# The gMLP's spatial part of a gated S4 and gMLP kernel: tokens instead of features on partitions, and an order of instructions that is written out

## The chip, the core and the metric

The kernel runs on one core of one Trainium2 chip, in bfloat16 with float32 accumulation in PSUM. The metric is the device time of one execution in microseconds, as the median of three runs. The engines are named as the profile names them: PE (TensorE, with its weight loads apart as PEld), DVE (VectorE), ACT (ScalarE), POOL (GpSimd) and SP (SyncE, which here only issues transfers).

## The reference

Two mixers read the same x of 2048 tokens by 640 features, and a gate for each token mixes what they give:

```python
def _A_ref(u, ...):                       # S4: a long convolution
    P = exp(dt * A * l)                   # 640 features x 128 states x 2048 positions, complex
    K = einsum('dn,dnl,dn->dl', C, P, dt * B).real
    y = irfft(rfft(pad(u)) * rfft(pad(K)))[:2048]
    return y + u * Dskip

def _B_ref(x, w_in, w_sp, b_sp, w_out):   # gMLP
    z = gelu(x @ w_in)                    # 2048 x 1728
    z1 = z[..., :864]
    z2 = layernorm(z[..., 864:])
    g = einsum('ts,bsf->btf', w_sp, z2) + b_sp[None, :, None]
    return (z1 * g) @ w_out               # 2048 x 864 by 864 x 640

g = sigmoid((x * gate_w).sum(-1, keepdims=True))
out = g * a + (1 - g) * b
```

The change is in the last three lines of `_B_ref` and in the half of z that is z1: w_sp is 2048 by 2048, b_sp has one number for each token, and z1 and g are 2048 by 864.

## The kernel before, in words

**How the order of instructions comes about.** The kernel first describes its work as some 1,700 tasks, with `Plan.add`: a task has one or several engines that may do it, a planned cost, the data it reads and writes, and the buffers it holds. `Plan.run` then plays the tasks through by these costs: whenever an engine comes free, it takes the task of the highest priority (the longest chain of planned costs that still hangs on it, plus a bias) whose inputs are ready and whose buffers are free. A table `TUNE` adds further biases to single calls. The result is one list of tasks, each with its engine. The instructions are issued in the order of this list, so each engine's queue is in order and has this fixed sequence; semaphores between engines follow from the data. The same holds for the queues of transfers, SP's and POOL's: a transfer whose data aren't ready holds up those behind it in its queue.

**Buffers.** PSUM has three rings of two buffers: `two` for pairs of banks (products of z1 and z2, the table products ps_k, the wide products of the convolution), `x` (ps_o, ps_s1x, ps_v) and `g` (ps_g, some ps_u). The rings in SBUF that matter here are wT (2), z1t (2), vT (4), br (2), ob (2) and zt (2, the staging of z1).

**The stages, with their lines in the profile.**

- x is loaded transposed; the z2 half of `x @ w_in` comes first (`z2_tile`, L592, tokens on partitions, two products of 432 columns for each slice of 128 features of x), with gelu and the layernorm's statistics on ACT and DVE. The normalised z2n stays in SBUF: 16 tiles of 128 tokens by 864 features.
- `z1_tile` (L624) makes z1 with features on partitions: for a group of 512 tokens, pairs of feature tiles of 128 (the last is 96), so products of 512 columns with the weights w_in as the stationary operand. ACT applies the gelu, and z1 goes to DRAM (z1_d) in two pieces for each pair, one for each block of 256 tokens. Of the four groups of 512 tokens two are made early, two between the tables of the S4 kernel.
- `s1_u` (L651, L655) is the first stage of the Fourier transform of u; its output goes from PSUM by copies (L422) to SBUF and to DRAM.
- `k_exps` and `k_tables` make, for eight slices of 80 features, tables of powers of the exponentials: angles on DVE and POOL (L361, L968, L993), sines and exponentials on ACT (L415), products on DVE (L1017 to L1028). `k_sub` (L1045, L1046) contracts each slice's tables over the 128 states in 160 small products ps_k; `k_store` and `k_expand` write the kernel K to DRAM and read it back widened.
- `conv_s1` (L1134, ps_s1k) transforms K, after the sixth ps_k for the first 480 features and after the eighth for the other 160. `conv_s2` multiplies the two spectra: ps_u (L1181) and ps_s2k (L1188) on PE, their product p on DVE (L1190, 32 wide ones of 2 x 480 columns, 16 narrow ones of 2 x 320), ps_v (L1196) on PE, and a copy on ACT (L1198). `conv_vt` (L1204) turns the result in 32 by 32 blocks with 16 transposes on DVE; `conv_i2` (L1278) ends the inverse transform. There the output is put together by L1212 on DVE (`stt`: gate times PSUM plus b) or by ACT and an addition (L1229, L1231), and stored.
- `sp_block(tb)`, for eight blocks of 256 tokens, is the spatial part. Two blocks are described ahead of the tables, two after them, four before `conv_s2`; where they run is up to the planned order, which fills PE's gaps with them.

**The spatial part before.** w_sp's rows for 256 tokens are loaded transposed into wT (16 slices of 128 source tokens by 256). Features are on partitions: for each of seven feature tiles, 16 products accumulate ps_g over the source tokens, with a tile of z2n as the stationary operand and 256 columns of wT as the moving one:

```python
pe.matmul(ps()[0:fs, ft - f0, :], lhsT=z2n[:, st, 128 * ft:128 * ft + fs], rhs=wT()[:, st, :], ...)      # L812
vec.tensor_tensor(out=v_, in0=ps, in1=br()..., op=ALU.add)                                                # L816
vec.tensor_tensor(out=v_, in0=v_, in1=z1t()..., op=ALU.mult)                                              # L818
```

b_sp varies along the columns here, so it is read as a row that is repeated over the partitions (br, loaded from a small table br_d in DRAM), and VectorE needs two operations for each pair of feature tiles, an addition from PSUM (L816) and a product with z1 (L818), 32 of each. Their result vT already has features on partitions and is the stationary operand of the last product ps_o (L832, 7 feature tiles, twice 320 columns for each 128 tokens). ps_o is scaled by 1 - gate into ob on DVE or ACT (L361, L836) and stored to DRAM (ob_d), or for the last four tiles of tokens kept in SBUF (acc).

## Time and profile before

| | |
|---|---|
| runs | 357.02, 362.8 and 356.61 us, median 357.02 |
| profiled execution | span of 353.6 us from the first to the last instruction |
| PE | 309.6 us busy in 3231 instructions, 88% of the span |
| DVE | 286.4 us in 548, 81% |
| ACT | 241.8 us in 437, 68% |
| POOL | 153.6 us in 155, 43% |
| ps_g, L812 | 896 instructions of 256 columns, 106.8 us of PE busy |
| L816 | 32 additions on DVE with 18.7 us busy |
| ps_o, L832 | 224 instructions of 320 columns, 34.3 us of PE busy |
| transfers | 59.89 MB, mean 169 GB/s |
| mean granted TensorE clock | 0.972 of full speed |

The page counts an engine as busy while at least one of its instructions is under way. On PE these overlap: the mean of one product in its group is the time from its start to its end, not the time from one product to the next. The page gives the span of the profiled execution; a run's time is the device's, and the three above are of other executions.

### The profile page before, as it was taken

How to read it: one execution, taken by the hardware profiler on the slowest of the kernel's cores; microseconds unless marked ns; L12 is line 12 of the kernel's file. 1: busy time of each engine (PE TensorE's matmuls, PEld its weight loads, DVE VectorE, ACT ScalarE, POOL GpSimd, SP SyncE). 2: the span in 40 equal slices, each digit the busy share in tenths (PEclk: the TensorE clock that was granted, in tenths of full speed). 3: DMA queues.
4: the chain of work that ended last, by engine and by line, in shares of the span. 5: the costliest groups of instructions: out<-in, count | busy, mean ns of one | idle time of the engine just before them, and what ended most of it. 6: DMA issues, size and time to landing. Idle time of an engine off the chain costs nothing.

```text
span 353.6 us, 8393 instructions
## 1 busy us (share of the span) xinstructions
PE 309.6 (88%) x3231; PEld 216.9 (61%) x3237; DVE 286.4 (81%) x548; ACT 241.8 (68%) x437; POOL 153.6 (43%) x155
## 2 busy tenths in 40 slices
PE   3899899989899999999699998699999999809982
PEld 3455445857778687878577776477774444405751
DVE  4079996789897949998489758777789999996985
ACT  1658975999784676889876684564538888804842
POOL 3005544600095826773187989434459400203221
PEclk9999999999999999999899999899999999977998
DMA  7988999669981578496592249998958886273404
GB/s 200 205 141 230 199 188 213 193 154 191 249 135 49 135 173 164 114 223 104 152 250 82 61 63 174 197 264 267 230 161 250 222 238 195 61 211 138 141 28 130
DMA packets 110809, 59.89 MB, mean 169 GB/s; under 512 B 78322, under 2 KB 107354, under 8 KB 110770
## 3 DMA queue, kind: packets, MB, share of 16 engines
q1 hardware_dynamic: 108530, 55.33, 63.9%
q0 software_dynamic: 2240, 4.04, 5.4%
q8 instruction: 25, 0.41, 0.5%
q14 instruction: 14, 0.11, 0.1%
HBM read 25.25 MB, written 19.47 MB: 126 GB/s over the span
## 4 chain that ended last, share of the span: by engine, by line
PE 44%; DVE 24%; ACT 10%; issue 7%; DMA 6%; POOL 5%; SPq 2%; ACTq 0%; DVEq 0%; POOLq 0%
PE ps_g L812 13%; DVE p L1190 5%; DVE vs L1204 5%; PE ps_z L592 5%; PE ps_o L832 4%; PE ps_z L624 4%; DMA xf<-in_A_u_dram 4%; PE ps_s2k L1188 3%; POOL ci L361 3%; PE ps_k L1045 3%; PE ps_v L1196 3%; PE ps_k L1046 3%; PE ps_s1k L1134 2%; ACT z2n L596 2%; ACT ET L415 2%
## 5 line engine op out<-in xcount | busy, mean ns | idle before, releaser
L812 PE MATMUL ps_g<-wT,z2n 128*128 128x256 bf16 (+1 forms) x896 | 106.8, 276 | 5.8 <-issue 2.8
L812 PEld LDWEIGHTS <-z2n 128*128 128x128 bf16 (+1 forms) x896 | 90.2, 103 | 22.7 <-issue 8.7
L1190 DVE TENSOR_TENSOR p<-ps_s2k,us 128x960 bf16<-128x960 f32 (+1 forms) x48 | 48.4, 1040 | 1.9 <-PE ps_s2k L1188 0.6
L361 POOL TENSOR_SCALAR ci<-ai 128x640 int32<-128x640 int32 (+1 forms) x8 | 21.5, 2693 | 55.3 <-DVE ai L968 33.2
L361 POOL TENSOR_SCALAR si<-th 128x80 int32<-128x80 f32 x40 | 32.1, 802 | 12.7 <-DVE t3p L761 4.6
L832 PE MATMUL ps_o<-Wout,vT 128*128 128x320 bf16 (+1 forms) x224 | 34.3, 299 | 3.0 <-ACT ob L836 3.0
L624 PE MATMUL ps_z<-xg,Win 128*128 128x512 bf16 (+1 forms) x134 | 31.6, 380 | 0.8 <-ACT zt L415 0.5
L592 PE MATMUL ps_z<-Win,xT 128*128 128x432 bf16 (+1 forms) x160 | 30.4, 346 | 2.1 <-ACT gl L598 2.1
L415 ACT ACTIVATE ET<-ci 128x640 bf16<-128x640 int16 (+1 forms) x40 | 26.0, 677 | 6.9 <-POOL ci L361 3.5
L832 PEld LDWEIGHTS <-vT 128*128 128x128 bf16 (+1 forms) x224 | 21.8, 98 | 13.5 <-issue 4.1
L1045 PE MATMUL ps_k<-ET 128*32 128x33 bf16 x640 | 27.7, 259 | 1.6 <-DVE ET L1028 1.1
L1045 PEld LDWEIGHTS <-ET 128*32 128x32 bf16 x640 | 26.9, 193 | 3.6 <-DVE ET L1028 3.1
L1198 ACT CAST vs<-ps_v 128x480 bf16<-128x480 f32 (+1 forms) x48 | 24.3, 521 | 5.1 <-PE ps_v L1196 4.1
L1046 PE MATMUL ps_k<-ET 128*32 128x33 bf16 x640 | 27.6, 258 | 0.0
L1046 PEld LDWEIGHTS <-ET 128*32 128x32 bf16 x640 | 27.1, 195 | 0.3 <-issue 0.3
L816 DVE TENSOR_TENSOR vT<-ps_g,br 128x512 bf16<-128x512 f32 (+1 forms) x32 | 18.7, 615 | 9.8 <-PE ps_g L812 9.8
L1188 PE MATMUL ps_s2k<-fk,T 128*128 128x480 bf16 (+1 forms) x128 | 25.0, 304 | 1.5 <-DVE p L1190 1.4
L1196 PE MATMUL ps_v<-p,G 128*128 128x480 bf16 (+1 forms) x128 | 25.1, 304 | 0.5 <-DVE p L1190 0.2
L592 PEld LDWEIGHTS <-xT 128*128 128x128 bf16 x160 | 15.5, 98 | 16.3 <-issue 3.0
L415 ACT ACTIVATE mr<-lre 128x320 bf16<-128x320 f32 x66 | 25.1, 457 | 0.0
L422 ACT CAST us<-ps_u 128x480 bf16<-128x480 f32 (+1 forms) x48 | 24.0, 521 | 0.7 <-ACT vs L1198 0.4
L415 ACT ACTIVATE ET<-ai 128x640 bf16<-128x640 int16 (+1 forms) x24 | 15.2, 645 | 12.1 <-DVE ai L968 12.1
(195 smaller groups left out, 618.7 us busy)
## 6 DMA issues: line engine op xcount, KB each, us to landing
FU_d<-s1u SPq DMA_DIRECT2D x16, 240.0 KB, 3.4
fu<-FU_d SPq DMA_DIRECT2D x16, 240.0 KB, 3.9
fk<-FK_d SPq DMA_DIRECT2D x16, 240.0 KB, 3.5
z_d<-zt SPq DMA_DIRECT2D x24, 128.0 KB, 2.5
z1t<-z_d SPq DMA_DIRECT2D x8, 384.0 KB, 4.3
xf<-in_A_u_dram SPq DMA_DIRECT2D x8, 320.0 KB, 3.4
Win<-in_B_w_in_dram SPq DMA_DIRECT2D x2, 1080.0 KB, 6.2
ob_d<-ob SPq DMA_DIRECT2D x12, 160.0 KB, 3.3
```

Source lines behind the costliest of these rows:

```text
L361: eng.tensor_scalar(out=out_, in0=in_, scalar1=s1, scalar2=None, op0=op0)
L415: return add("ACT", cost, lambda e: act.activation(out=out_(), in_=in_(), func=func, scale=scale), r=r, w=w, fset=fs, bias=bias, deps=deps ...
L592: pe.matmul(ps()[:, h, 0:432 + h], lhsT=xT[:, i, 128 * st:128 * st + 128], rhs=Win2[:, i, 432 * h:432 * h + 432 + h], start=(i == 0), stop ...
L624: pe.matmul(ps()[0:fs, ft - f0, :], lhsT=Win1[:, i, 128 * ft:128 * ft + fs], rhs=xg()[:, i, :], start=(i == 0), stop=(i == ND - 1))
L812: pe.matmul(ps()[0:fs, ft - f0, :], lhsT=z2n[:, st, 128 * ft:128 * ft + fs], rhs=wT()[:, st, :], start=(st == 0), stop=(st == NS - 1))
L832: pe.matmul(ps()[:], lhsT=vT[ft // 2]()[0:fs, ft % 2, 128 * r:128 * r + 128], rhs=Wout[0:fs, ft, HD * h:HD * h + HD], start=(ft == 0), sto ...
L1045: pe.matmul(o_, lhsT=ET[:, 0:32, d], rhs=M2[:, :, d], start=True, stop=False, tile_position=(0, 32 * q))
L1046: pe.matmul(o_, lhsT=ET[:, NA:NA + 32, d], rhs=E2[:, :, d], start=False, stop=True, tile_position=(0, 32 * q))
L1188: pe.matmul(ps()[:, i, W * n:W * n + W], lhsT=TK(k + n, i), rhs=fk()[:, j + n, :], start=True, stop=True)
L1190: add("DVE", dv1(2 * NW), lambda e, p12=p12, ps=ps, us=us: vec.tensor_tensor(out=p12()[:, :, 0:NW], in0=ps()[:, :, 0:NW], in1=us()[:, 0:NW ...
L1196: pe.matmul(pv()[:, W * n:W * n + W], lhsT=GV(k + n, i), rhs=p12()[:, i, W * n:W * n + W], start=(i == 0), stop=(i == 1))
L1198: add("ACT", 0.15 + NW / 1170, lambda e, k=k, pv=pv: act.copy(out=X["vs"][h][:, k:k + NK, :], in_=pv()[:, 0:NW].rearrange("p (k d) -> p k ...
```

## The change

**z1 with tokens on partitions.** `z1_tile` now makes 128 tokens at a time: x is the stationary operand and w_in the moving one, in two products of 432 columns for each slice of 128 features of x. One store of 216 KB follows for each tile of 128 tokens.

**The spatial part with tokens on partitions.** For each of the 16 tiles of 128 tokens, ps_g is made in two halves of 432 features, with wT as the stationary operand and z2n as the moving one. b_sp is now one number for each partition (bsf, a float32 copy of the tile bs16 in SBUF), so one operation adds it and multiplies by z1. The result v has tokens on partitions. PE turns it in seven transposes of 128 by 128 into PSUM (ps_vt, in the ring `x`), ACT or DVE copies the 896 columns to vT, and ps_o goes on as before. The seventh transpose takes features 736 to 863, so 32 features of the sixth come again; w_out's last tile lies in partitions 32 to 127, and its first 32 rows are zero.

**Buffers and transfers.** The rings are z1t (3), v (2) and vT (2) in place of z1t (2), vT (4) and br (2). The table br_d, its making and its eight loads are gone.

**The order.** `Plan.run` no longer plays anything through, and `TUNE` is gone. A string ORDER names every task and its engine, and the tasks are issued so. The whole sequence thus differs, not the spatial part's alone: the list puts ps_g, the z1 tiles, the tables and the convolution in other places, gives single copies to other engines, and begins "AS2AD4AY1AV1AX1AW1Dq1AU3". Some planned costs in the description differ too; with the list written out they decide nothing. The copy at L993 may no longer go to POOL.

```diff
-TUNE = {
-    ('conv_s1', 18, None): -5520,
...
+ORDER = """
+AS2AD4AY1AV1AX1AW1Dq1AU3Ac0Ad0Ae0Af0AC4Ag0Ah0AA4Aa0Ab2Am0AT1Dr1Ak1AB4AJ4Ai0AN1AZ2An2Ao2Aj0AK4Dp1As0Ds1AI4Dt0AE4AH4Ap1DH5AQ3DM1Cn4AF4AR4A20Aq1Cq4Du1Cl1
...
     def run(self):
         T = self.tasks
...
+        order = [(num(k), int(text[k + 2])) for k in range(0, len(text), 3)]
...
+        for i, e in order:
+            t = T[i]
...
+            t["fn"](self.ENG[e])
...
-    z1_d = dram.tile([8, P, NFT, 256], BF, name="z1_d")
+    z1_d = dram.tile([NS, P, Fh], BF, name="z1_d")
...
-    br_d = dram.tile([NS, P], BF, name="br_d")
...
-    for nm, n in (("dummy", 1), ("kk", 1), ("ti", 2), ("two", 2), ("g", 2), ("x", 2), ("wT", 2), ("z1t", 2), ("vT", 4), ("ob", 2), ("br", 2),
+    for nm, n in (("dummy", 1), ("kk", 1), ("ti", 2), ("two", 2), ("g", 2), ("x", 2), ("wT", 2), ("z1t", 3), ("v", 2), ("vT", 2), ("ob", 2),
...
+    add("DVE", 0.2, lambda e: vec.tensor_copy(out=bsf[:], in_=bs16[:]), r=["bs16"], w=["bsf"], bias=1000)
...
-            for ft in fts:
-                for i in range(ND):
-                    pe.matmul(ps()[0:fs, ft - f0, :], lhsT=Win1[:, i, 128 * ft:128 * ft + fs], rhs=xg()[:, i, :], start=(i == 0), stop=(i == ND - 1))
...
+            for i in range(ND):
+                for h in range(2):
+                    pe.matmul(ps()[:, h, 0:432], lhsT=xg()[:, i, 128 * j:128 * j + 128], rhs=Win1[:, i, 432 * h:432 * h + 432], start=(i == 0), stop=(i == ND - 1))
...
-        for b in range(2):
-            E(dma("SP", lambda b=b: z1_d[2 * g + b, 0:fs, f0:f0 + nf, :], lambda b=b: zt()[0:fs, 0:nf, 256 * b:256 * b + 256], 512 * fs * nf, r=[zt], w=[("z1", 2 * g + b, f0)], bias=5000, run=512 * nf))
...
+        E(dma("SP", lambda: z1_d[n], lambda: zt()[:].rearrange("p h f -> p (h f)"), 221184, r=[zt], w=[("z1", n)], bias=5000, run=1728))
...
-    dma("SP", lambda: Wout[0:96, 6, :], lambda: B_w_out[768:864, :], 123000, w=["Wout1"], r=["Win1"], bias=900, run=1280)
+    add("DVE", 0.2, lambda e: vec.memset(Wout[0:32, 6, :], 0.0), w=["Wout2"], bias=100)
+    dma("SP", lambda: Wout[32:128, 6, :], lambda: B_w_out[768:864, :], 123000, w=["Wout1"], r=["Win1"], bias=900, run=1280)
...
     def sp_block(tb):
...
+        FT0 = [128 * k for k in range(6)] + [736]
         for r in range(2):
             n = 2 * tb + r
+            z1t = sbt(lambda: gsp, "z1t", "z1t", [P, Fh], bufs=3)
+            dma("SP", lambda z1t=z1t, n=n: z1t()[:], lambda n=n: z1_d[n], 221184, r=[("z1", n)], w=[z1t], bias=1000 - 100 * tb, run=1728)
+            v_ = sbt(lambda: gsp, "v", "v", [P, Fh])
+            for h in range(2):
+                ps = gps("ps_g", [P, 512])
+                for c0 in range(0, NS, 4):
+                    def m(e, h=h, ps=ps, c0=c0, r=r):
+                        for st in range(c0, c0 + 4):
+                            pe.matmul(ps()[:, 0:432], lhsT=wT()[:, st, 128 * r:128 * r + 128], rhs=z2n[:, st, 432 * h:432 * h + 432], start=(st == 0), stop=(st == NS - 1))
...
+                add("DVE", dv1(432), lambda e, v_=v_, ps=ps, h=h, n=n, z1t=z1t: vec.scalar_tensor_tensor(
+                    out=v_()[:, 432 * h:432 * h + 432], in0=ps()[:, 0:432], scalar=bsf[:, n:n + 1], in1=z1t()[:, 432 * h:432 * h + 432], op0=ALU.add, op1=ALU.mult),
+                    r=[ps, z1t, "bsf"], w=[(v_, h)], bias=9500)
+            pt = xps("ps_vt", [P, 1024], BF)
+
+            def tr_(e, v_=v_, pt=pt):
+                for k in range(NFT):
+                    pe.transpose(out=pt()[:, 128 * k:128 * k + 128], in_=v_()[:, FT0[k]:FT0[k] + 128], identity=ident[:])
+            vT = sbt(lambda: gsp, "vT", "vT", [P, NFT * 128])
+            add("PE", NFT * mm(128), tr_, r=[(v_, 0), (v_, 1), "pre3"], w=[pt], hold_=[vT], bias=-1000 + 8 - 100 * tb)
+            evac(("ACT", "DVE"), NFT * 128, lambda vT=vT: vT()[:], lambda pt=pt: pt()[:, 0:NFT * 128], [pt], [vT], bias=9500)
...
-                        pe.matmul(ps()[:], lhsT=vT[ft // 2]()[0:fs, ft % 2, 128 * r:128 * r + 128], rhs=Wout[0:fs, ft, HD * h:HD * h + HD],
-                                  start=(ft == 0), stop=(ft == NFT - 1))
...
+                        pe.matmul(ps()[:], lhsT=vT()[:, 128 * ft:128 * ft + 128], rhs=Wout[:, ft, HD * h:HD * h + HD], start=(ft == 0), stop=(ft == NFT - 1))
```

## The prediction

> **What bounds the kernel now.** I read the page's busy times first, then busy time by stage, then the list of waits, then the chain and the time line around the stage borders. Stage borders are taken where TensorE (PE) finishes the sixth table product ps_k (203 us), where it starts the first ps_s2k (263 us) and where VectorE (DVE) ends the 32 wide products p (304 us). Columns of the table by stage, the second fence: stage, its length, then busy us and count of PE, weight loads, DVE, ACT, POOL, granted clock, DMA share, GB/s.
>
> ```profile
> PE 309.6 (88%) x3231; PEld 216.9 (61%) x3237; DVE 286.4 (81%) x548; ACT 241.8 (68%) x437; POOL 153.6 (43%) x155
> ```
>
> PEld is the loading of weights. The table by stage:
>
> ```profile
> 20.00:63.00 43.00, 41.34 (x225) 22.03 (x225) 37.67 (x86) 31.29 (x62) 17.87 (x14) 1.00 0.91 200
> 63.00:105.00 42.00, 38.09 (x317) 30.88 (x314) 36.82 (x75) 38.29 (x68) 11.88 (x14) 1.00 0.83 182
> 105.00:160.00 55.00, 53.72 (x938) 43.00 (x940) 47.83 (x99) 38.70 (x63) 34.55 (x27) 1.00 0.63 145
> 160.00:203.00 43.00, 39.39 (x561) 31.48 (x561) 33.25 (x66) 33.60 (x65) 26.63 (x17) 0.96 0.53 126
> 203.00:263.00 60.00, 54.50 (x674) 42.43 (x674) 43.26 (x84) 33.40 (x50) 35.53 (x41) 0.97 0.81 197
> 263.00:304.00 41.00, 39.42 (x197) 18.11 (x195) 40.11 (x46) 34.94 (x68) 13.14 (x18) 1.00 0.72 206
> 304.00:354.00 50.00, 30.22 (x253) 20.84 (x250) 41.32 (x56) 22.85 (x53) 10.37 (x11) 0.86 0.41 122
> ```
>
> Up to 203 us PE leads: it is busy 41.34 of 43 and 53.72 of 55 us, while DVE has gaps. From 263 to 304 DVE leads with 40.11 of 41. The last 50 us are DVE's too, with PE idle for 20.
>
> ```profile
> DVE vT L816 <- PE ps_g L812: 9.8, 8, 3.0
> ...
> DVE s1u L422 <- PE ps_s L651: 5.4, 2, 5.2
> ...
> DVE ET L993 <- PE ps_k L1046: 5.2, 3, 2.2
> ```
>
> These waits (waiter, releaser, total us, times, longest) say what DVE's gaps before 263 us are: DVE mostly waits for PE, whose queue is in order. And the chain's stretches in which nothing interrupts PE (start, length, what, count) give its real pace:
>
> ```profile
> 15.31 14.91 PE ps_z L592 x80
> ...
> 94.21 7.15 PE ps_g L812 x64
> ...
> 318.81 1.76 PE ps_i L1278 x4
> ```
>
> A 432-column product comes every 14.91/80 = 186 ns, a 256-column one every 7.15/64 = 112 ns (both near 2.3 columns per ns). By the same reading in the time line a 320-column one costs 136 ns (14 in 1.91), a 480-column one 203 ns (4 in 0.81), one ps_k 22 ns (160 in 3.54). The means near 300 ns in the page's groups are latencies of overlapping instructions. By this pace PE's whole work is 296 us; the rest of the 353.6 is waiting: 22 before 203 us (10 of it before the first z2 product), 7 in the next stage, 6 in 263 to 304, 22 after.
>
> The profiled execution has a span of 353.6 us. The three runs are 357.02, 362.8 and 356.61, so the two low ones lie 3.0 to 3.4 above the span; I add 3.2 to my span.
>
> **The change, part by part.** *Products on PE.* ps_g goes from 896 x 112 = 100.1 us to 512 x 186 = 95.4 (-4.7). z1 goes from 140 of 512 columns (15 in 3.25, 217 ns: 30.4) to 160 of 432 (29.8): -0.6. New are 112 transposes of 128 x 128. A lower bound is half a 256-column product, 56 ns (6.3 us together); the upper bound is the same operation in this trace, a row of PE's time line (start, length, what),
>
> ```profile
> 5.98 3.56 PE L557 MATMUL pt_s<-ident 128*128 128x128 bf16 x32
> ```
>
> 111 ns each, 12.4 us. That row is PE's first work, and the ten z2 products after it still need 2.10 us where ten later need 1.86, so I lean to the low end: 70 ns, 7.8 us. PE's total becomes 296 - 5.3 + 7.8 = 298.5: unchanged. The Trainium skill's TensorE: Matmul & The Clock Gate (Part 4, PE-mode transpose) speaks against this part: it gives some 275 ns for a transpose inside a kernel and says that transposes don't keep the clock up. At that price they would add 30.8 us instead of 7.8, and the change would lose; the row above, 32 in 3.56 us, is far below it.
>
> *DVE.* Away go 32 additions (L816: 15.9 + 3.3 us busy) and 32 products (L818: 10.4 + 2.2): -31.8. In come 32 fused operations of 432 columns. The nearest row is the same kind, L1212, 128x480 from PSUM with a bf16 tensor, 704 ns: 0.65 us each, 20.8. Bounds: the plain addition's 684 ns for 512 scaled to 432 (0.58, 18.5) and 0.704 unscaled (22.5). Of the 16 copies of the turned block (896 columns) the new order gives DVE 7 and ACT 9; by L422's 960-column rows (1.15 on DVE, 0.96 on ACT) 1.07 and 0.90: +7.5 and +8.1. Other copies change hands, about +6 on DVE. DVE ends near 289 against 286.4, ACT near 246 against 242; POOL loses the 8.4 us copy at L993. No engine gets less work: whatever is won comes from the order.
>
> *Transfers.* The z1 stores become 16 of 216 KB, with rows of 1,728 bytes, in place of 32 pieces; the bias rows br (8 loads of 64 KB) go; SP's queue issues 204 plain transfers in place of 224, and the same 42 transposing ones. The z1 loads come earlier than their use. I cost all this at nothing: the queue's waits aren't on the chain before 263 us except for the xf loads, which the order now issues earlier. If z1t came late, the fused operation would hold DVE, and behind it everything up to the next ps_g.
>
> *The added waits.* PE now waits for a block's v, then for its copy. I summed PE's work that the order puts between: 7.3 us at least between a block's last ps_g product and its transposes, and 6 us or more from there to its ps_o, except for blocks 1, 14 and 15 (1.3 to 2.8). A copy takes 1 us, so the wait is covered, and a queue ahead of it on DVE or ACT of some us too. Without that cover each block would cost about 0.65 + 0.5 + 1 = 2 us on PE, 34 us over 16 blocks. The transposes take one of the two psX buffers, which ps_o, ps_s1x and ps_v share; behind them on PE stands ps_g, which uses other ones.
>
> *The order, stage by stage* (PE work before and after, by the paces above).
> Up to the sixth ps_k: ps_g -15.7 (648 x 112 to 304 x 186), ps_o -7.7 (140 to 84), z1 +2.5, transposes +3.9, others -0.4: 180.8 becomes 163.4. DVE's work there falls by only 2.7, from 161.7 to 159. If PE sets the stage, 203 becomes 186. If DVE keeps its share of 20 to 160 us (122.3 of 140, 87%), it is 196. Since DVE's gaps were waits for PE, I take 188.
> To the first ps_s2k: PE +2.9; the chain of stores and expanded reads between the sixth ps_k and ps_s1k (20 us now, 203 to 223) stays. 62 instead of 60: 250.
> The 32 wide products p: 52 ps_g (+9.7), all 16 narrow ps_s1k (+2.2) and 7 transposes (+0.5) move in beside them, PE 34.8 to 47.2; DVE 43. PE becomes the bound, and the 41 us become 48: 298.
> The rest: PE had stood idle for 9.34 us here while 12 transposes ran on DVE (L1204). DVE has 16 narrow p (12.9), 16 transposes (18.7), 16 operations L1212 (7.8) and 7 additions of 0.4 (2.8) left: 42.2, against 41.32 now, then the last store (350.0 to 353.6): 45.8, with little waiting 46, against 50. Span 344, time 347.
>
> **The rivals.** *It cancels* (span 351, time 354). The 15 us off PE's early queue come back in the 7 us that the p stage grows by, and DVE holds the first stage to 196 at its present share, with 48 at the end: 196 + 62 + 48 + 46 is 352. For it: equal totals on all engines. Against: the list of waits above.
> *A tighter packing* (span 333, time 336). PE has 298.5 us of work, 10 of start, and some 15 idle in DVE's tail; if the other waits fall from 25 to 10 us, 333 is left. For it: between 20 and 160 us PE already ran at 95% of busy. Against: DVE, at 289 plus its 14 us of start, would have only 30 idle us in the whole span.
> *The tail decides* (span 364, time 367: slower). Now DVE has 11.9 us of work after its last p (338.1 to 350.0). The new order puts 10 of the 16 transposes (11.7), all 16 operations L1212 (7.8) and 7 additions (2.8) behind it: 22.3. If the p's end no earlier than now, because PE's extra 12.4 us in the p stage slow each p, the end moves by 10.4 us. It decides as soon as the last p comes later than 353.6 - 3.6 - 22.3 = 328 us; the sum above has it near 318. For it: PE's in-order queue now mixes blocks of 0.75 us of ps_g with the p chain. Against: 10 us less PE work before it.
> *It doesn't do what it says*: the fused operation is slower from PSUM than the row says, 0.9 us; 8 us more on DVE, a part of the second rival's loss.
>
> **How the numbers follow.** Forecast (336.5 to 350): 0.45. Tighter packing: 0.14. Cancelling: 0.22. Tail, or another loss of over 2%: 0.19. 2% of 357.02 is about what a measurement of this kernel can tell from no change, so faster means under 349.9 and slower over 364.2. Faster: 0.45 less a rim of 0.02 above 349.9, plus 0.14: 0.57. Same: 0.22 plus that 0.02, less a rim of 0.02 of the cancelling case above 364.2: 0.22. Slower: 0.19 plus 0.02: 0.21. The bounds of the transposes (-1.5 to +4.6 us), the fused operation (-2.3 to +1.7) and the first stage (186 to 196) give 336 to 356 for the likeliest case alone; the tail and the tighter packing widen the range to 332 to 365.
>
> **What would show it.** The sixth ps_k ends near 188 us and the first ps_s2k near 250. In the p stage PE, not DVE, is full. The 112 transposes take 0.4 to 0.8 us for 7. The fused operation takes 0.6 to 0.7 us. The last p ends near 318, and from there DVE runs without gaps to the last store. I am wrong if the sixth ps_k stays past 196 (DVE or ACT bound it, not PE), if PE waits for vT or v, or if the last p comes after 328.

## The result, and the profile after

The changed kernel takes 347.52 us, the median of four executions (346.8 to 349.56). The kernel before took 356.81 us in four executions on the same chip (355.52 to 362.8). The ratio is 0.9734, with a 95% interval of 0.9682 to 0.9785: faster by 2.7%. Ratios here are taken of undisturbed executions, so some differ a little from the quotient of two medians.

The profiled execution is the slowest of the four: 349.56 us, with a span of 347.8. The other three have spans of 345.0 to 346.1, so the stage times below are some 2 us more than a usual execution's.

From the page of the changed kernel, the engines' busy time and the granted TensorE clock in 40 slices of 8.7 us (in tenths):

```profile
PE 311.6 (90%) x2984; PEld 187.0 (54%) x2984; DVE 287.9 (83%) x530; ACT 245.1 (70%) x442; POOL 127.8 (37%) x148
...
PEclk9999999999989999999999978599999999999987
```

As forecast, no engine has less work (PE 309.6, DVE 286.4, ACT 241.8 before); only POOL lost 26 us. What the 9 us came from must therefore be waiting. The clock falls a little in slice 12, clearly in slices 24 to 26, between 200 and 226 us, and again at the end.

Busy time by stage of the changed kernel, cut where PE ends the sixth ps_k (182.4), starts the first ps_s1k (205.2) and the first ps_s2k (249.3), where the wide products p end (300.4) and where the last p ends (318.5). Columns as in the prediction's table:

```profile
...
20.00:60.00 40.00, 39.67 (x217) 21.10 (x216) 35.16 (x80) 29.57 (x61) 15.85 (x17) 1.00 0.94 205
60.00:95.00 35.00, 30.20 (x182) 16.04 (x183) 33.08 (x60) 34.73 (x61) 15.54 (x16) 1.00 0.79 188
95.00:140.00 45.00, 42.95 (x670) 28.50 (x669) 42.89 (x81) 35.38 (x60) 26.66 (x16) 0.96 0.65 140
140.00:182.00 42.00, 40.73 (x662) 27.18 (x662) 40.49 (x79) 37.41 (x67) 26.60 (x26) 1.00 0.53 133
182.00:205.00 23.00, 19.44 (x140) 11.30 (x132) 19.14 (x43) 13.48 (x22) 13.47 (x19) 0.97 0.89 138
205.00:226.00 21.00, 17.74 (x358) 12.07 (x359) 7.10 (x8) 5.66 (x10) 6.61 (x10) 0.66 0.73 182
226.00:249.00 23.00, 23.00 (x141) 12.94 (x140) 17.01 (x34) 14.72 (x19) 6.80 (x9) 0.96 0.73 201
249.00:300.00 51.00, 50.22 (x274) 25.69 (x273) 42.73 (x47) 39.43 (x74) 9.54 (x16) 1.00 0.81 225
300.00:319.00 19.00, 14.58 (x167) 11.86 (x166) 19.00 (x23) 12.18 (x32) 0.00 (x0) 1.00 0.53 160
319.00:348.00 29.00, 19.59 (x127) 12.27 (x124) 21.23 (x33) 11.85 (x23) 4.74 (x9) 0.87 0.30 91
```

Set against the prediction and the kernel before, the stages are these (us):

| stage | before | predicted | after | difference to predicted |
|---|---|---|---|---|
| to the sixth ps_k | 203 | 188 | 182.4 | -5.6 |
| to the first ps_s2k | 60 | 62 | 66.9 | +4.9 |
| the wide p | 41 | 48 | 51.1 | +3.1 |
| the rest | 50 | 46 | 47.4 | +1.4 |
| span | 353.6 | 344 | 347.8 | +3.8 |

Against the kernel before, the first stage won 20.6 us and the rest 2.6; the two stages between them gave 17 of that back. In the first stage PE and DVE are now nearly full at once (153.6 and 151.6 of 162 us between 20 and 182; DVE had 122 of 140 before), and ACT is busy for 137.1 of these 162 us. From 205 to 226 the clock is at 0.66 and DVE has 7 us of work. From 249 to 300 PE is full (50.22 of 51).

The new operations of the changed kernel, groups of instructions with shapes kept apart (busy us, mean ns of one | idle before, and what ended it):

```profile
L627 DVE SCALAR_TENSOR_TENSOR v<-ps_g,bsf,z1t 128x432 bf16<-128x432 f32 x32 | 21.0, 658 | 2.2 <-PE ps_g L623 2.2
L634 PE MATMUL ps_vt<-ident,v 128*128 128x128 bf16 x112 | 8.9, 219 | 0.0
L240 ACT COPY vT<-ps_vt 128x896 bf16<-128x896 bf16 x9 | 8.1, 900 | 3.9 <-PE ps_vt L634 3.9
L240 DVE COPY vT<-ps_vt 128x896 bf16<-128x896 bf16 x7 | 4.3, 616 | 1.1 <-PE ps_vt L634 1.1
```

The fused operation takes 658 ns, the seven copies on DVE 616 ns. PE's transposes never waited for v (the group's idle time is 0.0).

PE's time line of the changed kernel (start, length, what, count, idle time before in brackets) shows a set of transposes, then three stops (ahead of the first ps_s1k and among the ps_k) that several experiments below are about, and the last ps_o:

```profile
73.30 0.55 PE L634 MATMUL ps_vt<-ident,v 128*128 128x128 bf16 x7
73.69 0.89 PE L623 MATMUL ps_g<-z2n,wT 128*128 128x432 bf16 x4
...
205.19 0.96 PE L947 MATMUL ps_s1k<-xk,F 128*128 128x480 bf16 x2 [3.74 <-issue]
...
216.78 0.30 PE L858 MATMUL ps_k<-ET 128*32 128x33 bf16 x4 [0.58 <-issue]
...
222.16 0.30 PE L858 MATMUL ps_k<-ET 128*32 128x33 bf16 x4 [2.49 <-issue]
...
329.70 1.74 PE L646 MATMUL ps_o<-Wout,vT 128*128 128x320 bf16 x7 [2.10 <-ACT tm L1042]
331.24 2.56 PE L1095 MATMUL ps_i<-Wout,HT 128*128 128x256 bf16 x12
333.63 0.57 PE L1091 MATMUL ps_i<-vs,HT 128*128 128x480 bf16 x2
```

Seven transposes take 73.69 - 73.30 = 0.39 us of PE's queue, 56 ns each. At 205.19 PE has been idle for 3.74 us, at 222.16 for 2.49; "issue" means that the profile shows nothing it waited for. L1095 are 12 products whose result nobody reads: they are there to keep PE busy.

### The profile page after: what moved, and what is told of

It reads as the page before. It is cut to its first block, busy times and chain, and to the rows that moved or that the text cites. A ratio compares the mean times of both kernels' runs of the same rounds, so it can differ in the third digit from the quotient of the medians.

```text
span 347.8 us, 7804 instructions
## 1 busy us (share of the span) xinstructions
PE 311.6 (90%) x2984; PEld 187.0 (54%) x2984; DVE 287.9 (83%) x530; ACT 245.1 (70%) x442; POOL 127.8 (37%) x148
## 3 DMA queue, kind: packets, MB, share of 16 engines
q1 hardware_dynamic: 105126, 56.20, 66.9%
## 4 chain that ended last, share of the span: by engine, by line
PE 47%; DVE 31%; issue 7%; DMA 7%; ACT 5%; SPq 2%; DVEq 0%; ACTq 0%
PE ps_g L623 11%; PE ps_z L408 9%; DVE p L1003 7%; PE ps_o L646 6%; PE ps_z L438 4%; DVE vs L1017 3%; PE ps_s1k L947 3%; PE ps_k L858 3%; PE ps_s2k L1001 3%; DVE ET L841 3%; PE ps_k L859 2%; DVE ai L774 2%; PE ps_v L1009 2%; ACT ET L233 2%; DVE v L627 2%
## 5 line engine op out<-in xcount | busy, mean ns | idle before, releaser
L623 PE MATMUL ps_g<-z2n,wT 128*128 128x432 bf16 x512 | 105.3, 350 | 3.0 <-DVE v L627 2.7
L623 PEld LDWEIGHTS <-wT 128*128 128x128 bf16 x512 | 50.1, 99 | 47.9 <-issue 8.0
L646 PE MATMUL ps_o<-Wout,vT 128*128 128x320 bf16 x224 | 37.9, 314 | 4.8 <-ACT tm L1042 2.1
L180 POOL TENSOR_SCALAR ci<-si 128x640 int32<-128x640 int32 x14 | 29.9, 2140 | 17.7 <-DVE si L814 10.3
L408 PE MATMUL ps_z<-Win,xT 128*128 128x432 bf16 (+1 forms) x160 | 32.1, 358 | 0.0
L438 PE MATMUL ps_z<-Win,xg 128*128 128x432 bf16 x160 | 32.1, 356 | 0.0
L646 PEld LDWEIGHTS <-vT 128*128 128x128 bf16 x224 | 22.3, 102 | 16.9 <-issue 4.9
L858 PEld LDWEIGHTS <-ET 128*32 128x32 bf16 x640 | 27.2, 192 | 2.9 <-issue 1.5
L180 POOL TENSOR_SCALAR ci<-ai 128x640 int32<-128x640 int32 (+1 forms) x7 | 17.2, 2464 | 30.8 <-ACT ET L233 15.5
L180 POOL TENSOR_SCALAR si<-th 128x80 int32<-128x80 f32 x40 | 25.3, 633 | 4.3 <-DVE ai L781 1.8
L240 ACT CAST s1k<-ps_s1k 128x960 bf16<-128x960 f32 (+1 forms) x16 | 13.6, 859 | 15.6 <-PE ps_s1k L947 12.0
```

What stands on the lines that cost most here:

```text
L180: eng.tensor_scalar(out=out_, in0=in_, scalar1=s1, scalar2=None, op0=op0)
L240: (vec.tensor_copy if e == "DVE" else act.copy)(out=out_(), in_=in_())
L408: pe.matmul(ps()[:, h, 0:432 + h], lhsT=xT[:, i, 128 * st:128 * st + 128], rhs=Win2[:, i, 432 * h:432 * h + 432 + h], start=(i == 0), stop ...
L438: pe.matmul(ps()[:, h, 0:432], lhsT=xg()[:, i, 128 * j:128 * j + 128], rhs=Win1[:, i, 432 * h:432 * h + 432], start=(i == 0), stop=(i == N ...
L623: pe.matmul(ps()[:, 0:432], lhsT=wT()[:, st, 128 * r:128 * r + 128], rhs=z2n[:, st, 432 * h:432 * h + 432], start=(st == 0), stop=(st == N ...
L646: pe.matmul(ps()[:], lhsT=vT()[:, 128 * ft:128 * ft + 128], rhs=Wout[:, ft, HD * h:HD * h + HD], start=(ft == 0), stop=(ft == NFT - 1))
```

## The experiments

Three questions stood open after the result. Is it the layout or the written order that wins? What holds the first stage, which ended below the forecast although the forecast's bound (PE) was already its limit? And where did the 5 us of the second stage and the 3 us of the tail go?

### The layout or the order: two kernels under one planner

*planned_old_layout* is the kernel before with an empty TUNE, and with the planned costs of the changed description. *planned_new_layout* is the changed description, issued by the planner of the kernel before, also without TUNE. The two differ in the layout of the spatial part alone, as far as their planned order lets them.

```diff
 planned_old_layout:  -TUNE = { ... }            +TUNE = {}
                      (planned costs as in the changed kernel)
 planned_new_layout:  -ORDER = """AS2AD4..."""   +TUNE = {}
                      (Plan.run of the kernel before)
```

> The kernel before, planned by its own planner with an empty TUNE table and with the planned costs of the changed kernel. It is the partner of the next run: both layouts under one and the same untuned planner. Theory O (the order won the 9 us, the layout by itself nothing): slower than before by what the table was worth, 362 to 380 us, and within 2% of its partner. Rival L (the layout won it: 32 fused operations in place of 64, one store in place of two, no bias rows): its partner is faster by about 9 us.

> The changed kernel's description (tokens on partitions), but put in order by the planner of the kernel before with an empty TUNE table, not by the written list. Theory O: within 2% of the old layout under the same planner, so 362 to 380 us, slower than the kernel before. Rival L: 9 us faster than its partner, and near or below 357.

Measured: 388.39 us (385.12 to 392.15), 1.0756 times the kernel before (1.0668 to 1.0844), for the old layout; 384.88 us (382.68 to 385.72), 1.0716 times (1.0652 to 1.0781), for the new one. Both are slower than the 362 to 380 us expected; that they lie within 2% of each other is what theory O said. On the same scale the changed kernel stands at 0.9734. So of the step from 1 to 0.9734, leaving out TUNE and taking the other planned costs loses 0.076, the new layout under the same planner takes 0.004 (the intervals overlap), and the written list takes 0.098, some 35 us. Under this planner, then, the layout by itself does not bring the 9 us. These are not shares that add up by nature, since a list fits only the description that it was written for. Two things stay untested: what the planner would reach with a table tuned for the new layout, and how much of the list's gain is its choice of engines and not its order.

The pages say where the planner's orders lose. Old layout, then new, engines' busy time:

```profile
PE 317.6 (82%) x3237; PEld 218.4 (56%) x3237; DVE 290.3 (75%) x560; ACT 239.3 (62%) x426; POOL 153.1 (39%) x169
```

```profile
PE 311.9 (82%) x2984; PEld 182.9 (48%) x2984; DVE 287.2 (75%) x534; ACT 243.4 (64%) x432; POOL 155.0 (41%) x174
```

The new layout under the planner has the work of the changed kernel within 2 us on PE, DVE and ACT, and 33 us more span. Its sixth ps_k ends at 210.8 us, 28 later than the list's (the old layout's under this planner at 205.3), with DVE busy for 153.3 of 191 us from 20 on, that is 80%.

### The list on the old layout

The list was carried over to the old layout task by task: everything outside the spatial part keeps its place and its engine, the old ps_g, additions, products and ps_o take the places of the new ones, as far as data and buffers allow.

```diff
 kernel before:  -Plan.run's planned order, TUNE
                 +ORDER, the changed kernel's list with the old spatial tasks in the places of the new ones
```

> The old layout (features on partitions, addition and product apart) in the new order: every task that both kernels have stands in the changed kernel's list at the same place and on the same engine; the old spatial part's tasks take the places of the new ones (28 groups of four ps_g products spread over the places of 16, ps_o behind the block's last v, z1 tile for z1 tile). Theory O: most of the gain without the new layout, 346 to 352 us. Rival L: 357 or more, because DVE's 64 operations don't fit.

Measured: 410.1 us (406.35 to 411.57), 1.1413 times the kernel before (1.1332 to 1.1494). Both numbers were missed. The first stage ends more than 40 us later than under the list's own layout, so the waits lie in the places that the list had left for other operations. The run says that a list does not carry over. It does not say what a list written for the old layout would reach, so how much of the gain the new layout makes possible stays open.

### Taking the cover away

For the first 14 of 16 tiles the last fused operation, the transposes and their copy were moved to stand behind the tile's last ps_g in the list: directly in ten tiles, behind 2 to 16 other PE tasks in the tiles 5, 8, 10 and 11 (a task is, for example, four ps_g products). ps_o and its copies were moved up too. They follow the transposes at once, or nearly so, in the tiles 0, 1, 12 and 13; in the other ten 15 to 36 PE tasks stay between, since the store of an earlier ob stands ahead. So the cover of the transposes is taken, and that of ps_o only in part. The work is the same.

```diff
 order list, tiles 0 to 13:
-ps_g(n) last | ps_g, z1, s1_u, ps_k ... | transposes(n) | ... | ps_o(n)
+ps_g(n) last | v(n) transposes(n) copy(n) | ps_o(n) ob(n) (tiles 2 to 11: 15 to 36 PE tasks later) | ...
```

> The changed kernel with 14 of its 16 blocks' transposes, copies and ps_o moved directly behind the block's last ps_g group, so PE has no other work between ps_g, the transposes and ps_o. The prediction put the uncovered wait at 2 us on PE for a block (0.65 fused operation, 0.5 transposes, 1 copy): 14 blocks, 28 us, of which PE's idle time swallows some: 360 to 376 us. Rival: queues on DVE and ACT decide and PE's waits for v and vT are hidden all the same: under 351 us.

Measured: 406.04 us (405.16 to 406.94), 1.1316 times the kernel before (1.1256 to 1.1376), which is 58 us over the changed kernel and far outside both expectations. The prediction had put the price of missing cover at about 2 us for a block on PE, 28 for these 14. From the list of waits of this kernel (us in total, times, longest):

```profile
PEld L634 <- DVE v L627: 24.6, 15, 11.6
...
ACT vT L240 <- PE ps_vt L634: 21.5, 7, 6.0
PE ps_vt L634 <- DVE v L627: 20.6, 13, 11.1
...
DVE v L627 <- PE ps_g L623: 18.9, 11, 5.7
...
DVE ob L180 <- PE ps_o L646: 13.2, 7, 5.4
```

PE waits 20.6 us for v in 13 waits. One of them is 11.1 us; the other twelve are 0.8 each, near the 0.65 that the forecast had for v. For the copy PE waits 2.4 us only, since ps_o mostly does not follow it at once. But DVE and ACT, whose queues are in order too, now stand before v, the copy and ob until PE has come that far: DVE for 32 us in its two rows, ACT for 21.5 us before the copy. In the changed kernel DVE waits 2.2 us for v and ACT 3.9 us before the copy, so the cover works, and it covers three engines. What DVE owes to others then comes late: PE waits 10.8 us for the tables ET here, 0.8 in the changed kernel. Nearly all of the loss lies where the tiles were moved: the sixth ps_k ends at 228.1 us (45.7 later) and the next stage takes 77.5 us (10.6 more).

### Who holds the first stage: more PE, more DVE, less DVE

*more_pe_early* repeats the first four products of every ps_g half of the first eight tiles, 11.9 us more on PE before the sixth ps_k. *more_dve_early* does the fused operations of these eight tiles twice, 10.5 us more on DVE. *less_dve_early* gives four copies of 960 columns out of s1_u to ACT. Repeated work only overwrites its own result.

```diff
 more_pe_early, in front of a half's first ps_g:
+if c0 == 0 and tb < 4:
+    for st in range(4): pe.matmul(ps()[:, 0:432], ..., start=True, stop=True)
 more_dve_early:
-vec.scalar_tensor_tensor(out=v_()..., op0=ALU.add, op1=ALU.mult)
+[vec.scalar_tensor_tensor(out=v_()..., op0=ALU.add, op1=ALU.mult) for _ in range(2 if tb < 4 else 1)]
 less_dve_early, order list, four copies s1u<-ps_s:
-DVE
+ACT
```

> The changed kernel with the first four ps_g products of each half issued twice in the first eight tiles of tokens: 64 products of 186 ns more, 11.9 us of PE, all of it ahead of the sixth ps_k (which ended at 182.4 us). PE was idle for 8.4 of the 162 us from 20 to 182. Theory P (PE sets this stage, as the prediction had it): the sixth ps_k ends 6 to 12 us later, near 190, and the whole gets 6 to 12 us longer. Rival D (DVE sets it, PE only follows): under 3 us later.

> The changed kernel with the fused operation issued twice in the first eight tiles of tokens: 16 operations of 0.66 us more, 10.5 us of DVE, ahead of the sixth ps_k. DVE was idle for 10.4 of the 162 us from 20 to 182. Theory P: under 3 us later. Rival D: 6 to 10 us later. If both this and the run with more PE work are late by 6 us or more, the stage is full on both engines, and the forecast's reason, that DVE only waits for PE, was too simple.

> The changed kernel with four wide copies s1u of 960 columns (1.15 us each on DVE, 0.97 on ACT) moved from DVE to ACT, all ahead of the sixth ps_k, at the same places of the list: DVE 4.6 us less, ACT 3.9 us more. ACT was idle for 14 of the 87 us from 95 to 182. Theory D (since the run with more DVE work came out 8 us late and the one with more PE work 2: DVE now sets this stage): the sixth ps_k 2 to 4 us earlier, near 179, and the whole 1 to 4 us below 347.5. Rival P (PE sets it after all), or ACT's queue holds up the copies: sixth ps_k at 182 or later, time 347 or more.

Measured: more PE 349.45 us, the sixth ps_k at 186.1 (+3.7 for 11.9 us of work); more DVE 355.47 us, at 189.7 (+7.3 for 10.5); both one execution. How far the place of the sixth ps_k varies by itself can be read from the six profiles whose list is the same up to there (the changed kernel and five of the experiments below): 181.8 to 183.1. Both shifts are clear of that. Less DVE: 349.68 us (347.97 to 353.34), 0.9762 times the kernel before (0.9708 to 0.9816), against 0.9734 for the changed kernel, and the sixth ps_k at 184.6, later than in any of the six. The stretch from 20 us to the sixth ps_k in the first two kernels, by windows, each in a fence of its own:

```profile
20.00:186.00 166.00, 163.69 (x1797) 99.19 (x1795) 152.06 (x299) 138.07 (x247) 80.47 (x73) 1.00 0.71 160
```

```profile
20.00:190.00 170.00, 156.70 (x1738) 94.47 (x1736) 161.82 (x316) 139.11 (x248) 84.13 (x73) 0.99 0.67 156
```

and in the third the part of it after 60 us:

```profile
60.00:182.00 122.00, 112.86 (x1402) 69.86 (x1400) 111.00 (x209) 109.47 (x188) 65.34 (x58) 0.99 0.67 150
```

Each addition fills the engine that gets it to 95% or more (163.69 of 166 on PE, 161.82 of 170 on DVE) and only then lengthens the stage. An addition on DVE costs 0.7 of itself, one on PE 0.3, so DVE is nearer to the limit. But taking four copies of 1.15 us from DVE and giving them to ACT gained nothing: between 60 and 182 us DVE went from 116.5 to 111.0 us busy (part of that is work that slipped behind 182), ACT rose from 107.5 to 109.5 of 122 us, and DVE then waited 2.6 us for s1_u's products and 2.0 us for a set of transposes. That DVE alone sets this stage is not borne out by that. In the changed kernel PE and DVE are both close to full, each in a fixed sequence, and the one move that relieved DVE at ACT's cost gained nothing.

### The pause before the first ps_s1k

PE stands idle for 3.74 us ahead of the first narrow table transform. *gap_dummies* puts 20 products of 432 columns there whose result is overwritten. *gap_work* moves real work there: four ps_g products, three ps_o and their copies, and a store.

```diff
 gap_dummies, in front of the first ps_s1k:
+for k in range(20): pe.matmul(ps()[:, 0, 0:432], lhsT=f1(0), rhs=z2n[:, k % NS, 0:432], start=True, stop=True)
 gap_work, order list:
-ps_s1k | ps_o(8) | ps_s1k | ps_g(11) | ps_s1k | ps_o(8) | ps_s1k | ps_k ... ps_o(9)
+ps_g(11) | ob_d store(7) | ps_o(8) ob ps_o(8) ob | ps_o(9) ob | ps_s1k x4 | ps_k ...
```

> The changed kernel with 20 products of 432 columns, of no use, ahead of the first ps_s1k, where PE stood idle for 3.7 us (201.4 to 205.2) waiting for the reads xk and then ran for 6.8 us at half clock. Nothing else moves. Theory C (the idle time costs the clock, and the clock costs some 3 us of the 5 by which this stage was longer than forecast): granted clock 1.00 from 203 to 211, time 2 to 4 us below the changed kernel's 347.5. Rival X (the expanded reads set the pace, the clock is spare): within 1 us of 347.5. If the products overrun the wait: slower by up to 1 us.

> The changed kernel with four ps_g products and three ps_o (3.6 us by the row's paces), which stood behind the first ps_s1k, put ahead of it, with their copies on DVE and one store. Theory C: the clock stays at 1.00 and the useful work fills the idle time: 3 to 6 us below 347.5, first ps_s2k near 245. Rival X: the ps_s1k still wait for their reads, and what is won is given back before the first ps_s2k: within 1 us of 347.5.

Measured: dummies 346.6 us (343.19 to 348.14), 0.9673 (0.9607 to 0.9739); work 346.8 us (345.36 to 350.19), 0.9723 (0.9656 to 0.9791). Windows of 8 us around the pause, the changed kernel first, then the one with dummies:

```profile
196.00:204.00 8.00, 5.44 (x32) 2.69 (x29) 6.52 (x12) 2.90 (x4) 7.15 (x12) 0.98 1.16 191
204.00:212.00 8.00, 6.81 (x26) 3.33 (x26) 3.02 (x3) 2.05 (x3) 1.94 (x4) 0.59 0.92 193
212.00:220.00 8.00, 7.08 (x314) 6.75 (x313) 3.44 (x4) 2.84 (x6) 5.58 (x8) 0.84 1.03 277
220.00:228.00 8.00, 5.84 (x26) 2.85 (x26) 1.70 (x3) 1.73 (x3) 0.64 (x1) 0.52 0.09 28
```

```profile
196.00:204.00 8.00, 8.00 (x50) 4.41 (x49) 7.16 (x13) 2.91 (x4) 6.69 (x12) 1.00 1.12 192
204.00:212.00 8.00, 7.58 (x122) 4.86 (x124) 3.74 (x4) 4.03 (x6) 3.83 (x7) 1.00 1.14 216
212.00:220.00 8.00, 4.74 (x216) 4.50 (x211) 2.72 (x4) 0.87 (x3) 3.77 (x6) 0.67 0.96 284
220.00:228.00 8.00, 7.41 (x56) 4.10 (x56) 1.70 (x3) 2.71 (x5) 1.46 (x2) 0.69 0.14 47
```

The dummies remove the first stretch of low clock (0.59 becomes 1.00), and the first ps_s2k comes at 247.5 instead of 249.3. The second stretch stays (0.67 and 0.69), with two stops of 1.63 and 2.22 us between the ps_k. From the end of the sixth ps_k to the first ps_s2k it takes 64.8 us instead of 66.9. Two more profiles with the list of this stage unchanged, *less_dve_early* and *last_ps_o_earlier*, give 66.7 and 66.8, so the pause with its clock is worth some 2 us here. In the time it does not show: 346.6 is within 1 us of 347.5, and the intervals overlap. The first ps_s1k came at 205.8 with dummies, no earlier, so it is not PE's queue that sets it.

With real work ps_s1k came at 205.0, and then this happened on DVE (time line of *gap_work*):

```profile
206.53 0.55 DVE L180 TENSOR_SCALAR ob<-ps_o,omg 128x320 bf16<-128x320 f32 x1 [1.77 <-DMA ob_d<-ob]
...
207.47 1.15 DVE L240 CAST s1k<-ps_s1k 128x960 bf16<-128x960 f32 x1
```

The third ob copy, moved too early, waited 1.77 us for a store to free its buffer, the copy of ps_s1k stood behind it on DVE, and PE waited 2.56 us for that copy. Still, its first ps_s2k came at 246.8, and the stage took 64.3 us. The time is 0.7 us below 347.5, not the 3 to 6 expected. The moved step needs its buffer as well as its input.

### The long stretch of ps_k

In the changed kernel the 320 products of the seventh and the eighth slice stand in one stretch. *ps_k_apart* moves one ps_o, four ps_g products and a fused operation between the two slices.

```diff
 order list:
-ps_k(7) | ps_k(8) | v(11) | ps_o(9) | ... | ps_g(12)
+ps_k(7) | v(11) | ps_o(9) ps_g(12) | ps_k(8) | ...
```

> The changed kernel with seven ps_o products and four ps_g products put between the seventh and the eighth burst of ps_k, which stood back to back from 212.2 to 222.5 with two stops of 0.6 and 2.5 us in which PE waits for nothing the profile shows, the longer one beside the second stretch of half clock (217.4 to 227.6). Theory F (640 short instructions in a row outrun the loading of PE's own instructions, which then costs the stop and the clock): no stop over 1 us, the half-clock stretch shorter by 3 us or more, first ps_s2k 2 to 4 us earlier, time 1 to 3 us below 347.5. Rival (the stop comes from the transfers' load at that time, wherever the ps_k stand): the stop stays, time within 1 us.

Measured: 345.3 us (344.19 to 345.7), 0.9651 times the kernel before (0.9608 to 0.9694). Its windows at the same places:

```profile
212.00:220.00 8.00, 7.83 (x294) 6.87 (x289) 3.44 (x4) 2.06 (x5) 4.99 (x8) 1.00 0.98 273
220.00:228.00 8.00, 6.70 (x38) 3.00 (x38) 1.70 (x3) 3.55 (x5) 1.46 (x2) 0.57 0.29 78
```

Between 212 and 220 PE is busy for 7.83 us at full clock instead of 7.08 at 0.84. The stop inside the ps_k is 1.46 us instead of 2.49, and the first ps_s2k comes at 247.1, 2.2 us earlier, which is what the time shows too (345.3 against 347.52, on another chip; the intervals of the two ratios just overlap). The stage takes 64.2 us instead of 66.9. The stop became shorter and did not go, and the clock still falls. That it is at 1.00 up to 220 is not the cut's doing: in *last_ps_o_earlier*, where the stretch is whole, it is 1.00 from 212 to 220 too.

### The last ps_o

In the changed kernel's tail DVE waits 2.26 us for the first wide ps_i, which stands on PE behind the last ps_o and 12 filling products (the end of PE's time line above). *last_ps_o_earlier* moves that ps_o and three copies ahead of the last stage of ps_i.

```diff
 order list:
-ps_i ... | ob(14) ob(15) | ps_o(15) | ob(15)
+ob(14) ob(15) | ps_o(15) | ob(15) | ps_i ...
```

> The changed kernel with its last ps_o moved ahead of the four groups of ps_i for the narrow features, with the ACT copies that free its buffer. In the changed kernel that ps_o waited 2.1 us for a buffer (327.4 to 329.7), ran at half clock, and with the 12 warming products behind it kept the first wide ps_i back to 333.6, while DVE stood idle from 332.4 to 334.6. Theory T (this wait sets the end): the end 2 to 3 us earlier, 344.5 to 345.5. Rival (DVE's and ACT's remaining work sets the end): under 1 us.

DVE's time line, first of the changed kernel, then of this one:

```profile
331.73 0.65 DVE L1025 SCALAR_TENSOR_TENSOR wT<-ps_u,gsb,wT 128x160 bf16<-128x160 f32 x2
334.64 0.72 DVE L1025 SCALAR_TENSOR_TENSOR wT<-ps_i,gsb,wT 128x480 bf16<-128x480 f32 x1 [2.26 <-PE ps_i L1091]
```

```profile
332.68 0.70 DVE L1025 SCALAR_TENSOR_TENSOR wT<-ps_u,gsb,wT 128x160 bf16<-128x160 f32 x2
333.27 0.74 DVE L1025 SCALAR_TENSOR_TENSOR wT<-ps_i,gsb,wT 128x480 bf16<-128x480 f32 x1
```

Measured: 347.76 us (345.49 to 348.53), 0.9706 (0.9645 to 0.9768): no change that the interval can tell. The wait is gone, and from the last p to the end it takes 27.0 us instead of 29.3. But most of these 2.3 us are the changed kernel's profiled execution alone: there the last ps_o and the 12 products ran at half clock, from 330.0 to 333.4. In four other profiles with the same tail (*gap_dummies*, *gap_work*, *less_dve_early*, *ps_k_apart*) DVE waits 0.60 to 0.63 us at this place, and the tail takes 27.6 to 27.7 us. The row of *ps_k_apart*:

```profile
330.78 0.72 DVE L1025 SCALAR_TENSOR_TENSOR wT<-ps_i,gsb,wT 128x480 bf16<-128x480 f32 x1 [0.61 <-PE ps_i L1091]
```

So the move is worth 0.6 to 0.7 us, which these times can't show, and theory T fails. The second stage of this execution took 66.8 us, as in the changed kernel, although its stop among the ps_k was 4.69 us long: the length of the stop alone does not set the stage.

### Three moves together

The pause with a smaller move (four ps_g and two ps_o, without the third ob copy), the ps_k stretch and the last ps_o, in one list.

```diff
 order list:
+ps_g(11) ps_o(8) ob ps_o(8) ob ahead of the first ps_s1k
+v(11) ps_o(9) ps_g(12) between ps_k(7) and ps_k(8)
+ob(14) ob(15) ps_o(15) ob(15) ahead of the last stage of ps_i
```

> Three moves in the order list at once: gate products ps_g of a block in the pause before the first narrow table transform ps_s1k, other gate work between the eighth slice's small products ps_k so that they don't stand in one stretch, and the last ps_o of the spatial part ahead of the last wide ps_i. Theory, the pauses are separate and each costs what its own run gave: 1 us from the pause (first ps_s2k 246.8 alone), 2.2 us from the ps_k stretch (first ps_s2k 247.1 alone), 1 to 2 us in the tail: first ps_s2k at 244 to 246, last p to end 27 us, span 341 to 343, time 343 (342 to 345). Rival, behind them stands one and the same limit, the reads of the expanded K and DVE: then the first ps_s2k comes no earlier than 246.5, and the time is 345 to 347, as with the best single move.

Measured: 345.08 us (342.53 to 346.84) in six executions, 0.9563 times the kernel before (0.9498 to 0.9629). Its windows from the sixth ps_k (181.8) to 226:

```profile
182.00:205.00 23.00, 21.52 (x138) 12.63 (x136) 19.75 (x45) 12.98 (x22) 14.19 (x21) 1.00 0.92 143
205.00:226.00 21.00, 17.11 (x353) 11.08 (x354) 7.24 (x8) 7.48 (x13) 6.93 (x10) 0.84 0.80 185
```

The clock is 1.00 and 0.84 where the changed kernel had 0.97 and 0.66; the pause is 1.49 us instead of 3.74. The first ps_s2k comes at 245.9, the last p to the end takes 27.2 us, the span is 342.7: these numbers lie where the theory had them. Its reason is not borne out, though. The sixth ps_k ended 0.6 us early, before any of the moves, and from there the stage takes 64.1 us, where single moves gave 64.8, 64.3 and 64.2. So the pauses are not separate and the gains don't add; the rival's one limit behind them fits the stage better, though its bound of 246.5 was passed. Which limit it is stays open. The median time, 345.08, is at the theory's upper edge and as near to the rival's. The kernel before was slower on this chip than on the others (median 362.05), so the ratio is better than the time. By its ratio this version beats the changed kernel and, of course, the kernel before; by the time alone it can't be told from *ps_k_apart*. One stop of 2.73 us among the ps_k is still there.

## Why the prediction was right, and where it was right by luck

The time was 347.0 against 347.52 measured. Step by step it looks less good.

**The costs of the new operations.** The fused operation was put at 650 ns and took 658. The transposes were put at 70 ns, between bounds of 56 and 111, and took 56, the lower bound: 6.3 us in all instead of 7.8. The step that leaned upward was the two slower products behind the first transposes of the trace; it should have given way to the plain scaling by columns. In the groups the mean of one is 219 ns, which is a time from start to end; what the queue pays is the time line's 0.39 us for seven. The Trainium skill, TensorE: Matmul & The Clock Gate, has a figure near each: about 275 ns for a transpose in a kernel (Part 4: PE-mode transpose), and 55.6 ns from start to start for products of 128 columns at full clock (Part 1: The HAM clock gate). The measurement decides for the second. The granted clock stayed at 0.96 to 1.00 in the windows from 20 to 205 us, sets of transposes among them. The copies of the turned block on DVE were put at 1.07 us by a float32 row of 960 columns (1.15) and took 616 ns: a copy of bfloat16 out of PSUM isn't scaled from one of float32. That is 7 x 0.45 = 3.2 us less on DVE. The copies on ACT were right at 0.90. The totals were forecast at PE 298.5 by pace (the page's busy 311.6 against 309.6 before, so nearly unchanged, as said), DVE 289 (287.9), ACT 246 (245.1).

**The added waits.** The cover was there, as summed from PE's work between the steps. In the first stage PE waited 2.7 us for v, in two waits of ps_g for the buffer that v reads, and 1.0 us for vT in one of ps_o; the transposes waited for nothing. By its wording the sign "if PE waits for vT or v" came, but these 3.7 us are too little to decide anything. The price without cover was mis-sized: 34 us for 16 blocks counted PE's waits alone, and *no_cover* cost 58 for 14 (406.04 against 347.52), although it left part of ps_o's cover. Its list of waits shows DVE and ACT losing as much as PE.

**The first stage: 188 against 182.4.** The time was nearly right and the mechanism wrong. The step that failed is "Since DVE's gaps were waits for PE, I take 188": it held that PE sets the stage and DVE follows. DVE's share rose from 87% to 94%, and the end came below PE's bound of 186, since 3 of the 22 us of PE's waiting went too. Added work lengthened the stage by 0.3 of itself on PE and 0.7 on DVE, so PE does not set it alone. DVE's waits from 20 us to the sixth ps_k in the changed kernel, the longest of the list:

```profile
DVE ET L841 <- ACT ET L233: 1.4, 1, 1.4
DVE bst L420 <- ACT z2n L412: 1.3, 1, 1.3
DVE t3p L575 <- PE ps_z L438: 1.0, 1, 1.0
```

None is over 1.4 us, and waits for PE are no longer first. The kernel before had 5.4 us for s1_u and 5.2 for ps_k here, and 2.0 for ps_g (the other 7.8 us of the prediction's first row lie behind 203). What did this is the list that was written for this layout, not the layout by itself: the same description under the planner ends this stage at 210.8, the old layout under the planner at 205.3. The prediction had summed the order's work for each engine and could not see that the list would also close the gaps; it had that only as the rival "a tighter packing", with 0.14.

**The second stage: 62 against 66.9.** The step "the chain of stores and expanded reads ... stays" took over 20 us of chain and added 2.9 of PE work. That it stays failed by 2.7 of the 4.9 us: from the sixth ps_k to the first ps_s1k it took 22.8 us, 20.1 before. The three runs that put work into PE's pause there have 22.5 (*gap_work*), 23.1 (*gap_dummies*) and 23.2 (*three_moves*), so it is not PE's queue that made it longer; why it grew stays open. From there to the first ps_s2k it took 44.1 us, where the forecast leaves some 42. What was not priced is that less of PE's work was left to fill the stage: 17.74 of 21 us after 205, a pause of 3.74 before it, two stops of 0.58 and 2.49 us and, in the same stretch, half the clock for 17 us against 3.4 in the kernel before. The stage as a whole takes 66.7 to 66.9 us in the three profiles with its list unchanged and 64.1 to 64.8 in the four that moved or added PE work there. So 2 to 2.8 of the 4.9 us come back by any one of these moves, and no more by two of them together.

**The wide products: 48 against 51.1.** PE is the bound, as forecast. DVE waited 5.0 us for ps_s2k there, the longest of its waits. The paces held: ps_g took 183 ns and ps_s2k 204 ns from start to start in this stage. The term that was mis-sized is PE's sum of 47.2 us. By the forecast's own paces the products that the trace has there come to some 49 us (an estimate from the counts: 157 products of 480 columns, 53 of ps_g, 44 of 320, 12 of 160, 7 transposes), so more of PE's work lay in this stage than was summed. The other 2 us are small gaps between the products, 0.5 to 0.8 of them waits for p.

**The rest: 46 against 47.4.** The last p ended at 318.5, with 318 forecast. From there 22.3 us of DVE work and 3.6 to the last store were forecast, 25.9 in all; it took 29.3. DVE was busy for 21.7 of them, idle for 4.1 in four waits (2.26, 0.28, 0.79 and 0.79 us), and 3.5 us passed from its last operation to the end. "With little waiting" failed by these 4.1 us. Of the 2.26 behind the last ps_o some 1.7 belong to the half clock of this one execution: four other profiles have 0.60 to 0.63 there, and tails of 27.6 to 27.7 us.

**From span to time.** The 3.2 us added to the span were too much. They compared the span of one execution with the times of others; where span and time belong to the same execution, they differ by 1.7 to 1.9 us in all runs here (349.56 and 347.8, 345.7 and 343.9, 344.45 and 342.7).

So the forecast hit by luck in part: -5.6 in the first stage stood against +9.4 in the other three, which makes the span 3.8 us too short, and the constant added 3.2 us where 1.8 was due. The rest is that the longest of four executions was profiled, 2 us above the median. What was right for its own reason is that no engine's work shrinks, so that the gain had to be waiting, most of it in the first stage, and that part of it is lost again in the p stage.

**The rivals.** "It cancels" was right that the gain comes back in the p stage (10 us did) and wrong on the first stage, which did not end at 196. "The tail decides" was right on the amount of DVE work behind the last p; its point, a last p after 328, wasn't reached. The slow fused operation did not show.

## What to carry to other kernels

When a change swaps a layout and the whole order at once, run both layouts under one scheduler: here the layout changed the time by 0.4% under a planner that was tuned for neither, less than the intervals can tell, while the written list took some 35 us off that planner's order, and equal totals on all engines had said from the start that the gain had to be waiting. Price a wait in an in-order queue on both sides: taking the cover from 14 blocks cost 58 us, twice what the waiting engine's own count said. And when work moves out of a stage that has a fixed chain of transfers, look at what then fills the chain: up to 2.8 of the 4.9 us lost there against the forecast came back by moving a few products, whichever of the moves was made.
